# Gated linear attention plus a Fourier mix: rest rows stored in another order, z one step later, operands of the second product in other places

## The chip, the cores and the metric

The kernel runs on one core of a Trainium2 chip. The metric is device time in microseconds (us) of one execution. The engines are TensorE (PE; its weight loads are PEld), VectorE (DVE), ScalarE (ACT), GpSimd (POOL) and SyncE (SP, which only issues DMAs here; POOL issues some too).

## The reference

```python
x = A_x                                   # 1 x 2048 x 576
g = sigmoid((x * gate_w).sum(-1))         # a number per row
q, k, v = split(x @ wqkv)                 # 32 heads of 18
phi(t) = where(t > 0, t + 1, exp(t)) + 1e-6
kv  = phi(k)^T v ;  z = sum over rows of phi(k)
a   = ((phi(q) kv) / (phi(q) z + 1e-6)) @ wo
b   = dft_seq_re @ (B_x @ dft_hid_re^T) - dft_seq_im @ (B_x @ dft_hid_im^T)
out = g * a + (1 - g) * b                 # b uses x too (A_x)
```

`ORDER`, `PRODUCTS` and the "forms" below come from a scheme that multiplies 2 x 2 blocks with seven products instead of eight. All matmuls run in fp32r, each float32 operand split in a high part (`hi_of`, on ACT) and a low part (`lo_of`, on DVE), so that a product takes three passes (`FULL`).

## The kernel before

SBUF is one arena in which every tile has a byte address written by hand (`T_AT`, `ACC_AT`, `SLOT_AT`, ...). Where two tiles share bytes, the later writer waits until all readers of the earlier are done. SP runs in the order of the code, ACT and DVE from early in stage 1 on; PE's and POOL's order is chosen by the scheduler, PE's only up to the first product. Each DMA of SP takes one of eight lanes (a semaphore each, `DMAHW0` to `DMAHW7`) in turn, and waits until the DMA eight before it has landed.

The stages, with their places in the profiled execution:

1. k (0 to some 70 us): 16 row tiles of x times wk; `feature` gives k' in `acc[i]`, `pk[i]` holds its two parts. Beside it, `Left` makes the seven forms of x for the Fourier part, for 8 "pairs" of row blocks, and POOL stores them to DRAM (`xforms`, read back as `xf<-xm`). The 64 columns of x that don't fill a block of 128, the "rest", are made by `Left(NP)` for four pairs at once, in the two places g: a tile `plain` of 128 rows, q x r (32 rows of four pairs). SP stores it to `xrest` with six DMAs (L375), hi, hi and lo for each g; `load_rest` reads 96 rows of one pair (`xr<-xr`). This tile lies at `ACC_AT`, under `acc[0]` to `acc[5]`.
2. kv (to some 145 us): 20 steps (5 column chunks `c` of 4), each with 64 or 32 matmuls of `c` (x, loaded as `craw<-in_xg`) with `pk` (L599). Beside the steps: `zacc` sums k' over the tiles on DVE; `z_chain` splits the sum into `zs`, `z_sum` sums it over rows with four matmuls with `ones` (L197, tiles `zs`, `ones`) into `zb`; `kv_step` multiplies `gt` with `wv` (L581, L584); the five parts of `wo` are loaded (`wo_at`, one of them at the place of `zs`) and split; `wq` is loaded and split.
3. q (to some 226 us): 16 calls of `q_tile`: x times wq (28 matmuls, L197, tiles `wd`, `xs`), `feature` writes `acc[i]` (DVE, L331), and the next x is loaded (`xraw`, L247) and split (`xs`). After tile 1 `build_kv` masks kv; after tile 3 `build_m` multiplies it with `wo` into M (`mf`), all five groups; `move_m` brings M's rows to their places by POOL DMAs in the steps i = 4 to 6; `split_m` splits it after tiles 9 and 10. `wr_pieces` makes the forms of the Fourier weights.
4. attention (to 293.7 us): q' is normalised, transposed and multiplied with M; POOL stores `att`; the last forms of x are made (`Left(0)`, `Left(1)`, `Left(7)`), and `first` loads weights and x.
5. First product, `Hidden.run` (293.7 to 348.4 us): 8 pairs x 7 products x 7 matmuls (L857; the seventh is the rest). The results go to `Factors`, one of eight places `pair[p]` = `T_AT + p * TPAIR` for pair p. `load_x(p, k)` loads x's forms in four parts, `follow` says beside which pair's products the x of a later pair is loaded. `m.load(0)` loads the first 2 x 128 rows of the sequence matrix (`craw`), of which DVE and ACT make forms during pair 3.
6. First sequence (348.4 to 527.1 us): 32 steps `n` = (j, b), 168 matmuls each on average (L1018): matrix forms `c` with factors; step b uses pairs 2b and 2b + 1. `row` tiles (`att`) are loaded for each j, mixed, and stored (`mid`). `late(n)` makes the second weights and, in the last steps, starts the second product's loads.
7. Second product (527.1 to 587.3 us) and second sequence (to the end), with the imaginary matrices; `mid` takes the place of `att`, `out` that of `mid`.

The class `Layout` holds the addresses of the sequence matrix's batches, of x (`x`), rests (`rest`) and weights (`w`) for both products; `swap` is 1 for the second.

Of the kernel before, what the change touches and what calls it, by code (L numbers as in the profile page):

```python
# [8 lines left out]
F = mybir.dt.float32  # L9
# [5 lines left out]
P = 128  # L15
# [73 lines left out]
class Layout:  # L89
# [4 lines left out]

    def __init__(self, swap):
        self.swap = swap
        a, b = (2, 0) if swap else (0, 2)
        slot = [SLOT_AT + k * SLOT for k in range(7)]
        self.low = [slot[k] for k in (a + 1, b + 1, 4, 6)]
        self.high = [slot[k] for k in (a, b, 5)]  # L100

    def batch(self, n):

        if n == 0:
            return [T_AT + p * TPAIR for p in (NP - 2, NP - 1)]
        return self.low[(n - 1) % 4], self.high[(n - 1) % 3]

    def x(self, p, k):
        if 2 <= p <= 4:
            return T_AT + (4 * TPAIR, 7 * TPAIR, 4 * TPAIR + 7 * XF + XR)[p - 2] + k * XF  # L110
        return SLOT_AT + (p + self.swap) % 2 * 7 * XF + k * XF

    def rest(self, p):
        if p == 2:
            return T_AT + 4 * TPAIR + 7 * XF
        if p == 3:
            return T_AT + (NP - 2) * TPAIR + TPAIR // 2
        if p == 1 and not self.swap:
            return T_AT + 60416
        return WF_AT + 4 * WF if p % 2 else SLOT_AT + 14 * XF + 3 * WF  # L120

    def w(self, k):
        return WF_AT + k * WF if k < 4 else SLOT_AT + 14 * XF + (6 - k) * WF


@with_exitstack
def kernel(
# [209 lines left out]
    class Left:  # L337
# [18 lines left out]
        def make(self):  # L356

            r, c = self.f[:, :, 1], self.c
            add(r[:, 0], r[:, 1], r[:, 6])
            add(r[:, 4], r[:, 2], r[:, 6], ALU.subtract)  # L360
            yield
            add(r[:, 3], r[:, 0], r[:, 2], ALU.subtract)
            add(r[:, 6], r[:, 5], r[:, 3], ALU.subtract)
            yield
            hi_of(c[:, :4, 0], r[:, :4])
            hi_of(c[:, 4:, 0], r[:, 4:])
            yield
            for fs in (slice(0, 4), slice(4, 7)):
                lo_of(c[:, fs, 1], r[:, fs], c[:, fs, 0])
                if self.k < NP:  # L370
                    nc.gpsimd.dma_start(out=xforms[self.k][:, fs], in_=c.bitcast(F)[:, fs])
                yield
            for j in range(0 if self.k < NP else 6):
                k, g = j // 2, j % 2
                nc.sync.dma_start(out=xrest[g, :, k], in_=self.plain.bitcast(F)[:, g, k // 2])  # L375

    lefts = []

# [211 lines left out]
    for c in range(5):  # L590
        ps = [bank(), bank()]
        passes = FULL if c < KC else FULL[:2]
        for q in range(NCU):
# [129 lines left out]
        for o, s in todo:  # L723
            lo_of(o[:, :, 1], s, o[:, :, 0])

    def build_m():
        for g in range(NG):
# [90 lines left out]
    class Hidden:  # L818
# [38 lines left out]
                nc.tensor.matmul(ps, a, b, start=(start and n == 0), stop=(n == len(ops) - 1),  # L857
                                 skip_group_check=True)

        def run(self, m):  # L860
            rest = None

            follow, follow_rest = {0: 4, 2: 5, 3: 6, 5: 7}, {0: 4, 1: 5, 4: 6, 5: 7}
            self.load_rest(3)
            self.load_pair(3)
            for p in range(NP):
                fs = Factors(T_AT + p * TPAIR)
                factors.append(fs)
                t = fs.raw
                ys = (y_ring.next() for _ in range(3))  # L870
                if p == 0 and self.lay.swap:
                    o = self.lay.rest(3) + XR
                    ys = range(o, o + 3 * HALF * 4, HALF * 4)
# [202 lines left out]
    for i in range(NT):  # L1076
# [41 lines left out]
    def late(n):  # L1118
        k, part = divmod(n - 4, 7)
        if 0 <= k < 3 and part != 1:  # L1120
            go(wi_pieces[k])
        if 24 <= n < 28:
            second.load_w(n - 24)
        if n == 28:
            second.load_rest(1)
        if n == NP * NB - 3:
            second.load_rest(0)
            second.load_x(0, 4)
            second.load_x(0, 6)
            second.load_x(1, 0)  # L1130
        if n == NP * NB - 2:
            second.load_x(0, 0)
            second.load_x(0, 2)
            second.load_w(4)
        if n == NP * NB - 1:
            second.load_w(5)
            second.load_w(6)
            second.load_rest(2)
            for k in (2, 4, 6):
                second.load_x(1, k)  # L1140
# [19 lines left out]
def _layouts(inputs):  # L1160
# [14 lines left out]
    def left(xt):  # L1175
# [61 lines left out]
```

## Time and profile before

| what | us |
|---|---|
| median of 3 runs (lowest, highest) | 772.09 (768.91, 773.06) |
| profiled execution, own time | 771.09 |
| its span, first to last instruction | 769.4 |
| PE busy in the span | 732.4 |
| DVE, ACT, POOL busy | 600.7, 336.0, 56.7 |
| mean granted clock of PE (1 is full) | 0.980 |
| first product, second product | 54.7, 60.1 |

Rows of the timeline read: start, length, engine, line, operation, tiles; in brackets the idle time of the engine ahead of it and what ended that. Rows of waits: who waited for whom, us in total, times, longest. Rows of stretches: busy time and instructions of PE, PEld, DVE, ACT and POOL, then the granted clock, the busy share of the 16 DMA engines, and GB/s. Line numbers are those of the kernel before.

### The profile page before, as it was taken

The page shows a single profiled execution, that of the slowest core. Times are in us where ns is not written, and L with a number is a line of the kernel's source. Part 1 is how long each engine was busy: PE and PEld are TensorE (multiplying, and loading weights), DVE is VectorE, ACT ScalarE, POOL GpSimd, SP SyncE. Part 2 cuts the span into 40 slices and gives each one's busy share as a digit, 9 for nine tenths or more (in the row PEclk, how much of TensorE's full clock was granted, in tenths as well). Part 3 has the DMA queues.
Part 4 walks back from the last instruction along what each step waited for, and adds up shares of the span by engine and source line. Part 5 has one row for each costly group of instructions (what it writes and reads, how often), then busy time and mean ns, then how long its engine had stood idle before and what let it go on. Part 6 is the DMA issues. An engine that isn't in the chain of part 4 may idle for free.

```text
span 769.4 us, 13840 instructions
## 1 busy us (share of the span) xinstructions
PE 732.4 (95%) x5428; PEld 727.6 (95%) x5428; DVE 600.7 (78%) x993; ACT 336.0 (44%) x518; POOL 56.7 (7%) x98
## 2 busy tenths in 40 slices
PE   7999998539999999999999999999899999999998
PEld 7999998539999999999999999999889999999998
DVE  5789865236999985789998889885688987878885
ACT  6888435327864444435332424222343423333321
POOL 0111300005103211000001010000000000000000
PEclk9999999859999999999999999999999999999999
DMA  5476875226747797964547484868994354454441
GB/s 180 141 263 216 288 277 176 100 97 203 225 154 231 277 342 254 350 202 172 167 148 260 163 278 162 271 225 312 365 305 164 113 170 147 129 157 148 152 144 48
DMA packets 53724, 157.21 MB, mean 204 GB/s; under 512 B 6364, under 2 KB 10908, under 8 KB 52636
## 3 DMA queue, kind: packets, MB, share of 16 engines
q1 hardware_dynamic: 44412, 117.28, 46.4%
q0 software_dynamic: 8960, 38.65, 14.2%
q8 instruction: 43, 0.70, 0.4%
q10 hardware_dynamic: 288, 0.41, 0.1%
q14 instruction: 21, 0.17, 0.1%
HBM read 113.44 MB, written 41.39 MB: 201 GB/s over the span
## 4 chain that ended last, share of the span: by engine, by line
PE 71%; DMA 10%; DVE 2%; SPq 2%; issue 1%; ACT 0%; DVEq 0%; ACTq 0%
PE bank L1018 46%; PE bank L197 16%; PE bank L857 6%; DMA xf<-xm 4%; DMA xr<-xr 2%; DMA xraw<-in_xa_dram 2%; DMA mid<-row 1%; PE bank L695 1%; PE bank L599 1%; SPq L375 1%; DMA wraw<-in_wv_dram 1%; DMA xm<-xb 1%; SPq L247 1%; DVE fl L177 1%; DVE fl L187 0%
## 5 line engine op out<-in xcount | busy, mean ns | idle before, releaser
L1018 PE MATMUL bank<-fh,c 128*128 128x288 f32 x1792 | 357.6, 295 | 0.0
L1018 PEld LDWEIGHTS bank<-fh,c 128*128 128x128 f32 x1792 | 287.6, 188 | 0.0
L1018 PE MATMUL bank<-fl,c 128*128 128x288 f32 x896 | 264.4, 295 | 0.0
L167 ACT ACTIVATE c<-craw 128x1792 fp32r<-128x1792 f32 (+1 forms) x84 | 121.4, 1447 | 189.6 <-DVE craw L187 161.0
L1018 PEld LDWEIGHTS bank<-fl,c 128*128 128x128 f32 x896 | 168.9, 189 | 0.1
L197 PE MATMUL bank<-wd,xs 128*128 128x288 f32 (+1 forms) x896 | 128.1, 305 | 24.7 <-DVE acc L331 19.4
L197 PEld LDWEIGHTS bank<-wd,xs 128*128 128x128 f32 x896 | 125.2, 196 | 26.2 <-DVE acc L331 19.6
L177 DVE TENSOR_TENSOR c<-craw,c 128x1792 fp32r<-128x1792 f32 (+4 forms) x86 | 142.0, 1654 | 3.8 <-ACT c L167 3.6
L187 DVE TENSOR_TENSOR craw<-craw 128x256 f32<-128x256 f32 (+1 forms) x192 | 98.3, 512 | 34.1 <-DMA craw<-in_ci_dram 19.4
L857 PE MATMUL bank<-wf,xf 128*128 128x288 f32 x588 | 93.9, 300 | 4.1 <-ACT y L888 2.4
L857 PEld LDWEIGHTS bank<-wf,xf 128*128 128x128 f32 x588 | 84.8, 191 | 6.0 <-ACT y L888 3.0
L197 PE MATMUL bank<-mw,qs 128*128 128x288 f32 x448 | 63.3, 298 | 0.0
L599 PE MATMUL bank<-pk,c 128*128 128x288 f32 x448 | 62.7, 301 | 0.0
L331 DVE SCALAR_TENSOR_TENSOR acc<-bank,e 128x288 f32<-128x288 f32 x64 | 28.3, 454 | 43.4 <-DMA xraw<-in_xa_dram 23.1
L599 PEld LDWEIGHTS bank<-pk,c 128*128 128x128 f32 x448 | 61.3, 193 | 0.1
L197 PEld LDWEIGHTS bank<-mw,qs 128*128 128x128 f32 x448 | 60.0, 188 | 0.2 <-DVE qs L177 0.2
L187 DVE TENSOR_TENSOR ys<-bank,ys 128x288 f32<-128x288 f32 x63 | 28.8, 457 | 16.1 <-PE bank L1018 12.9
L167 ACT ACTIVATE fh<-fl 128x864 fp32r<-128x864 f32 (+1 forms) x32 | 29.8, 950 | 26.4 <-DVE fl L187 26.4
L329 ACT ACTIVATE e<-bank 128x288 f32<-128x288 f32 x64 | 25.9, 405 | 34.6 <-DVE acc L331 19.5
L177 DVE TENSOR_TENSOR fl<-fl,fh 128x864 fp32r<-128x864 f32 (+1 forms) x32 | 34.6, 1093 | 7.1 <-ACT fh L167 5.9
L857 PE MATMUL bank<-wf,xr 96*128 96x288 f32 x112 | 33.7, 301 | 2.3 <-DMA xr<-xr 2.3
L1083 ACT ACTIVATE acc<-bank,gate 128x288 f32<-128x288 f32 x32 | 16.0, 502 | 35.1 <-PE bank L197 34.8
(101 smaller groups left out, 622.0 us busy)
## 6 DMA issues: line engine op xcount, KB each, us to landing
xf<-xm SPq DMA_DIRECT2D x42, 512.0 KB
craw<-in_cr_dram SPq DMA_DIRECT2D x32, 512.0 KB
craw<-in_ci_dram SPq DMA_DIRECT2D x32, 512.0 KB
xraw<-in_xa_dram SPq DMA_DIRECT2D x31, 320.0 KB
xm<-xb POOLq DMA_DIRECT2D x8, 1024.0 KB, 5.4
wf<-wm SPq DMA_DIRECT2D x14, 576.0 KB
xm<-xb POOLq DMA_DIRECT2D x8, 768.0 KB, 5.5
xr<-xr SPq DMA_DIRECT2D x16, 336.0 KB
```

Source lines behind the costliest of these rows:

```text
L167: return nc.scalar.activation(dst, src, AF.Copy, bias=bias)
L177: nc.vector.tensor_tensor(out=dst, in0=src, in1=hi, op=ALU.subtract)
L187: nc.vector.tensor_tensor(out=dst, in0=a, in1=b, op=op)
L197: nc.tensor.matmul(ps, a, b, start=(n == 0), stop=(n == len(pairs) - 1))
L247: nc.sync.dma_start(out=raw, in_=xa[order.pop(0)])
L329: nc.scalar.activation(e, ps, AF.Relu, scale=-1.0)
L331: nc.vector.scalar_tensor_tensor(dst, ps, 0.0, e, op0=ALU.max, op1=ALU.add)
L375: nc.sync.dma_start(out=xrest[g, :, k], in_=self.plain.bitcast(F)[:, g, k // 2])
L599: nc.tensor.matmul(ps[h][:, :HALF], t[:, a, k], pk[s][:, b, half(h)], start=(s == 0 and n == 0), stop=(s == NT - 1 and n == len(passes) - 1))
L857: nc.tensor.matmul(ps, a, b, start=(start and n == 0), stop=(n == len(ops) - 1), skip_group_check=True)
L1018: nc.tensor.matmul(ps[q], c[x][:, l, k], factors[p](y, f), start=(p == 0 and i == 0), stop=(p == NP - 1 and i == 2))
L1083: done.append(nc.scalar.activation(acc[i][:, half(h)], ps[:, :HALF], AF.Copy, scale=gate[:, i:i + 1]))
```

## The change

Seven edits:

- Rest rows: x's rest is laid out so that a row of SBUF is r x q instead of q x r (the host gives `in_xq`'s rest block in that order), and the six stores write the same `xrest` with r as the outermost dimension.
- `z_chain` stands at the head of step 15's extra work instead of behind it; `z_sum`, the splits of `wo` and its loads come one step later.
- `Layout`: the same slots for the batches in both sequences; x's places in one table `xs`. In the second product x of pairs 0 to 4 lies in `pair[1]` to `pair[5]`, the places of the factors of the next pair; in the first, pairs 0 and 1 as before in the slots, 2, 3 and 4 in `pair[4]`, `pair[7]`, `pair[5]`. Rests get eight places: two of them beside what lies in `pair[6]`, one in `pair[7]`, the others in the ring of `row` tiles, behind the weights, and in slot 4.
- `late`: the second product's loads begin at step 27 (rest 0) and 28 (x of pair 0) instead of 28 and 29; in the last step x of the pairs 2 to 4, the rests up to 6 but 5, and `mi.load(0)` are put in SP's queue.
- First product: rest 2, x 3, rest 3, `mr.load(0)` and rest 4 stand ahead of the run. `follow` and `follow_rest` are given by the caller.
- The first two `wo` splits that were left are done in a loop behind `q_tile(0)`.
- `build_m` in three parts: groups 0 and 1 after tile 3, 2 and 3 after tile 4, 4 after tile 5.

```diff
 class Layout:
     def __init__(self, swap):
...
-        a, b = (2, 0) if swap else (0, 2)
         slot = [SLOT_AT + k * SLOT for k in range(7)]
-        self.low = [slot[k] for k in (a + 1, b + 1, 4, 6)]
-        self.high = [slot[k] for k in (a, b, 5)]
+        self.low, self.high = [slot[k] for k in (3, 1, 4, 6)], [slot[k] for k in (2, 0, 5)]
+        pair = [T_AT + p * TPAIR for p in range(NP)]
+        self.first = pair[6], pair[7]
+        self.xs = pair[1:6] if swap else [slot[0], slot[2], pair[4], pair[7], pair[5]]
+        self.xs += [slot[0], slot[2], slot[0]]
+        far, near = WF_AT + 4 * WF, slot[4]
+        self.sums = pair[7] + SLOT + XR
+        self.rests = [MIX_AT if p in (1, 7) else pair[6] + SLOT + (p - 2) * XR if p in (2, 3) else
+                      pair[7] + SLOT if p == 6 else far if p in ((0, 5) if swap else (4,)) else near
+                      for p in range(NP)]
...
     def x(self, p, k):
-        if 2 <= p <= 4:
-            return T_AT + (4 * TPAIR, 7 * TPAIR, 4 * TPAIR + 7 * XF + XR)[p - 2] + k * XF
-        return SLOT_AT + (p + self.swap) % 2 * 7 * XF + k * XF
+        return self.xs[p] + k * XF
...
-                nc.sync.dma_start(out=xrest[g, :, k], in_=self.plain.bitcast(F)[:, g, k // 2])
+                nc.sync.dma_start(out=xrest[g, :, k].rearrange("q r f n -> r q f n"),
+                                  in_=self.plain.bitcast(F)[:, g, k // 2])
...
+            if step == NT - 1:
+                z_chain()
             if q == 1 and c:
                 kv_step(c - 1)
...
-            elif step == NT - 1:
-                z_chain()
-            if step == NT:
+            if step == NT + 1:
                 z_sum()
-            if step >= NT:
+            if step > NT:
                 wo_split.pop(0)(lo_later)
-            if NT - 2 <= step < NT + 3:
-                g = step - NT + 2
+            if NT - 1 <= step < NT + 4:
+                g = step - NT + 1
...
-    wo_split.pop(0)()
+    for f in wo_split:
+        f()
...
-    build_m()
+    build_m((0, 1))
     for i in range(4, NT):
         q_tile(i)
+        build_m({4: (2, 3), 5: (4,)}.get(i, ()))
...
-            follow, follow_rest = {0: 4, 2: 5, 3: 6, 5: 7}, {0: 4, 1: 5, 4: 6, 5: 7}
-            self.load_rest(3)
-            self.load_pair(3)
...
-                    if p == 1 and k == 3:
-                        m.load(0)
...
-    hidden.load_rest(2)
...
         if 24 <= n < 28:
             second.load_w(n - 24)
+        if n == 27:
+            second.load_rest(0)
         if n == 28:
+            second.load_pair(0)
+        if n == 29:
+            second.load_pair(1)
             second.load_rest(1)
-        if n == NP * NB - 3:
...
+        if n == 30:
             second.load_w(4)
-        if n == NP * NB - 1:
             second.load_w(5)
+        if n == 31:
             second.load_w(6)
             second.load_rest(2)
+            second.load_rest(4)
             second.load_pair(2)
+            second.load_pair(3)
+            second.load_rest(3)
+            mi.load(0)
+            second.load_pair(4)
+            second.load_rest(6)
...
-    first.run(mr)
+    first.load_rest(2)
+    first.load_pair(3)
+    first.load_rest(3)
+    mr.load(0)
+    first.load_rest(4)
+    first.run(mr, {0: 4, 1: 5, 2: 6, 6: 7}, {0: 5, 3: 6, 4: 7})
...
-    second.run(mi)
+    second.run(mi, {1: 5, 2: 6, 6: 7}, {0: 5, 1: 7})
...
-        rest = rest.transpose(3, 1, 0, 2, 4).reshape(1, P, 4, 2 * P)
+        rest = rest.transpose(1, 3, 0, 2, 4).reshape(1, P, 4, 2 * P)
```

Where the order moves, engine by engine (line, operation, out<-in with numbers that tell tiles apart, size; in brackets the semaphores that an instruction waits for, where shown). First SP at the end of the kv stage, the loads of `wo` (L561) and the rest stores (L375), before:

```order
L561 DMA wraw_1541<-in_wo_dram 126x576
L498 DMA craw_1572<-in_xg_dram 128x512
L561 DMA wraw_1581<-in_wo_dram 126x576
L561 DMA wraw_1623<-in_wo_dram 126x576
L561 DMA wraw_1659<-in_wo_dram 126x576
L561 DMA wraw_1684<-in_wo_dram 72x576
L375 DMA xr_102<-xb_1223 4x32x896 x6
```

and after:

```order
L495 DMA craw_1569<-in_xg_dram 128x512
L558 DMA wraw_1578<-in_wo_dram 126x576
L558 DMA wraw_1611<-in_wo_dram 126x576
L558 DMA wraw_1654<-in_wo_dram 126x576
L558 DMA wraw_1679<-in_wo_dram 126x576
L371 DMA xr_102<-xb_1223 32x4x896 x6
L558 DMA wraw_1708<-in_wo_dram 72x576
```

The stores' shape changes from 4x32x896 to 32x4x896, and the last `wo` load moves behind them. DVE at the start of the q stage, where `acc_78` is `acc[0]`, before:

```order
L177 TENSOR_TENSOR gt_1712<-bank,gt_1712 128x288 [waits Activation_49] x2
L331 SCALAR_TENSOR_TENSOR acc_78<-bank,e_1744 128x288 [waits DMAHW2_49,DMAHW3_49,DMAHW1_49,DMAHW6_49,DMAHW0_49,DMAHW7_49,DVE_49,Activation_49]
L331 SCALAR_TENSOR_TENSOR acc_78<-bank,e_1764 128x288 [waits PE_49,Activation_49]
L653 TENSOR_SCALAR gate_75<-gate_75 128x1
L654 RECIPROCAL gate_75<-gate_75 128x1 [waits DVE_49]
L177 TENSOR_TENSOR xs_904<-xraw_905,xs_904 128x640 [waits Activation_49]
```

Nothing moves here: after the change the same instruction waits for six DMA lanes too. ACT at the end of the sum of k', before:

```order
L167 ACTIVATE c_1490<-craw_1488 128x512
L167 ACTIVATE plain_1502<-wraw_1503 128x576
L167 ACTIVATE zs_954<-zacc_953 128x576
L167 ACTIVATE xb_1223<-xb_1222 128x4x2x128
L167 ACTIVATE xb_1223<-xb_1222 128x3x2x128
```

and after:

```order
L163 ACTIVATE c_1490<-craw_1488 128x512
L163 ACTIVATE zs_954<-zacc_953 128x576
L163 ACTIVATE plain_1502<-wraw_1503 128x576
L163 ACTIVATE xb_1223<-xb_1222 128x4x2x128
L163 ACTIVATE xb_1223<-xb_1222 128x3x2x128
```

`zs` moves ahead of `plain` (the last chunk of `wv`). SP in the second product, from the load of x of pair 3 (`xm_97`) on, before:

```order
L833 DMA xr_6139<-xr_102 96x896
L840 DMA xf_6141<-xm_97 128x1024
L840 DMA xf_6143<-xm_97 128x1024
L840 DMA xf_6145<-xm_97 128x1024
L840 DMA xf_6147<-xm_97 128x512
L840 DMA xf_6176<-xm_98 128x1024
L840 DMA xf_6194<-xm_98 128x1024
L840 DMA xf_6214<-xm_98 128x1024
L840 DMA xf_6226<-xm_98 128x512
L833 DMA xr_6231<-xr_102 96x896
L954 DMA craw_6278<-in_ci_dram 128x1024
```

and after, where rest 4 (`xr_6118`) already stands ahead of x of pair 2:

```order
L839 DMA xf_6128<-xm_97 128x1024
L839 DMA xf_6130<-xm_97 128x1024
L839 DMA xf_6132<-xm_97 128x1024
L839 DMA xf_6134<-xm_97 128x512
L832 DMA xr_6136<-xr_102 96x896
L947 DMA craw_6138<-in_ci_dram 128x1024
L839 DMA xf_6140<-xm_98 128x1024
L839 DMA xf_6142<-xm_98 128x1024
L839 DMA xf_6144<-xm_98 128x1024
L839 DMA xf_6146<-xm_98 128x512
L832 DMA xr_6148<-xr_102 96x896
```

`craw` and the rest of pair 4 move ahead of x of pair 4 (`xm_98`).

More of the change, by code (lines that the diff above doesn't have):

```diff
@@ L96, in __init__ @@
         self.swap = swap
-        a, b = (2, 0) if swap else (0, 2)
         slot = [SLOT_AT + k * SLOT for k in range(7)]
-        self.low = [slot[k] for k in (a + 1, b + 1, 4, 6)]
-        self.high = [slot[k] for k in (a, b, 5)]
+        self.low, self.high = [slot[k] for k in (3, 1, 4, 6)], [slot[k] for k in (2, 0, 5)]
[8 more added lines that the diff above has]
+                      for p in range(NP)]
     def batch(self, n):
-        if n == 0:
-            return [T_AT + p * TPAIR for p in (NP - 2, NP - 1)]
-        return self.low[(n - 1) % 4], self.high[(n - 1) % 3]
+        return (self.low[(n - 1) % 4], self.high[(n - 1) % 3]) if n else self.first
     def x(self, p, k):
-        if 2 <= p <= 4:
-            return T_AT + (4 * TPAIR, 7 * TPAIR, 4 * TPAIR + 7 * XF + XR)[p - 2] + k * XF
-        return SLOT_AT + (p + self.swap) % 2 * 7 * XF + k * XF
+        return self.xs[p] + k * XF
     def rest(self, p):
[L114 to L120, printed above, removed]
+        return self.rests[p]
     def w(self, k):
-        return WF_AT + k * WF if k < 4 else SLOT_AT + 14 * XF + (6 - k) * WF
+        return WF_AT + k * WF if k < 4 else SLOT_AT + 14 * XF + XR + (6 - k) * WF
 @with_exitstack
@@ L724, in build_kv, with build_m @@
             lo_of(o[:, :, 1], s, o[:, :, 0])
-    def build_m():
-        for g in range(NG):
+    def build_m(gs):
+        for g in gs:
             n = gsize(g)
@@ L858, in product, with run @@
                                  skip_group_check=True)
-        def run(self, m):
+        def run(self, m, follow, follow_rest):
             rest = None
-            follow, follow_rest = {0: 4, 2: 5, 3: 6, 5: 7}, {0: 4, 1: 5, 4: 6, 5: 7}
-            self.load_rest(3)
-            self.load_pair(3)
             for p in range(NP):
@@ L871, in run @@
                 if p == 0 and self.lay.swap:
-                    o = self.lay.rest(3) + XR
-                    ys = range(o, o + 3 * HALF * 4, HALF * 4)
+                    ys = range(self.lay.sums, self.lay.sums + 3 * HALF * 4, HALF * 4)
                 p3, p2, e = (at(o, [P, HALF], F, "y") for o in ys)
@@ L1123, in late @@
             second.load_w(n - 24)
+        if n == 27:
+            second.load_rest(0)
         if n == 28:
+            second.load_pair(0)
+        if n == 29:
+            second.load_pair(1)
             second.load_rest(1)
-        if n == NP * NB - 3:
[L1127 to L1133, printed above, removed]
+        if n == 30:
             second.load_w(4)
-        if n == NP * NB - 1:
             second.load_w(5)
+        if n == 31:
             second.load_w(6)
             second.load_rest(2)
-            for k in (2, 4, 6):
-                second.load_x(1, k)
+            second.load_rest(4)
             second.load_pair(2)
-    paced.enter_context(tc.manual_schedule(engines={mybir.EngineType.PE}))
-    first.run(mr)
+            second.load_pair(3)
[3 more added lines that the diff above has]
+            second.load_rest(6)
+    paced.enter_context(tc.manual_schedule(engines={mybir.EngineType.PE}))
+    first.load_rest(2)
[4 more added lines that the diff above has]
+    first.run(mr, {0: 4, 1: 5, 2: 6, 6: 7}, {0: 5, 3: 6, 4: 7})
     sequence(mr, gate_n, att, mid, between=late)
     factors.clear()
-    second.run(mi)
+    second.run(mi, {1: 5, 2: 6, 6: 7}, {0: 5, 1: 7})
     sequence(mi, gate_m, mid, [out[t * P:(t + 1) * P] for t in range(NT)], last=gate_n)
```

## The prediction

> **What bounds the kernel now.** I read the page first, then who TensorE waited for, then busy time and clock by stretch, and then the order of time at each wait found.
>
> ```profile
> span 769.4 us, 13840 instructions
> PE 732.4 (95%) x5428; PEld 727.6 (95%) x5428; DVE 600.7 (78%) x993; ACT 336.0 (44%) x518; POOL 56.7 (7%) x98
> PEclk9999999859999999999999999999999999999999
> PE bank L197 <- DVE acc L331: 19.4, 1, 19.4
> ```
>
> TensorE is the bound: 95% busy, so only its 37 us of idle time and the time at a lower clock (eighth and ninth slice) can be won. Over half of the idle time is one wait of 19.4 us for the first write of `acc` in the q stage. The stretches around it (us; busy PE, PEld, DVE, ACT, POOL; clock; DMA share; GB/s):
>
> ```profile
> 128.00:131.40 3.40, 3.40 (x16) 3.40 (x16) 2.97 (x6) 2.14 (x6) 0.00 (x0) 0.51 0.02 9
> 145.90:165.40 19.50, 0.08 (x2) 0.05 (x1) 0.56 (x2) 0.07 (x1) 0.00 (x0) 0.57 0.37 140
> 165.40:172.40 7.00, 6.51 (x25) 6.15 (x26) 6.46 (x20) 3.88 (x11) 0.00 (x0) 0.50 0.02 7
> 172.40:176.00 3.60, 3.60 (x28) 3.60 (x28) 2.43 (x7) 2.40 (x6) 0.00 (x0) 0.99 0.30 91
> 144.00:146.00 2.00, 1.93 (x17) 1.70 (x15) 0.00 (x0) 1.32 (x4) 0.00 (x0) 1.00 0.26 106
> 318.00:320.00 2.00, 2.00 (x17) 2.00 (x16) 0.38 (x2) 0.41 (x1) 0.00 (x0) 1.00 1.01 262
> 298.00:300.00 2.00, 2.00 (x17) 2.00 (x16) 1.17 (x3) 0.41 (x1) 0.00 (x0) 1.00 1.05 422
> xr<-xb SPq DMA_DIRECT2D x6, 448.0 KB
> 132.92 15.37 SPq L375 DMA_DIRECT2D xr<-xb  x6
> 164.84 0.82 DVE L331 SCALAR_TENSOR_TENSOR acc<-bank,e 128x288 f32<-128x288 f32 x2 [23.15 <-DMA xraw<-in_xa_dram]
> ```
>
> From 145.9 to 165.4 no engine works; only DMAs run. SP issues the six rest stores (L375) from 132.92 on, and while they run alone (144 to 146) the DMA share is 0.26 of 16 engines, four engines, at 106 GB/s. 6 x 448 KB are 2.75 MB, 26 us at that rate, which fits the end of the wait. DVE's wait is labelled `xraw`, but its instruction in the order names six DMA lanes, those of the six stores: their source lies where `acc[0]` is written. After the idle time the clock is 0.50 until 172.4.
>
> **The change, part by part.**
>
> *A, the rest stores.* In the stretch 145.90 to 165.40 TensorE loses 19.4 us. From 165.40 to 172.40 it issues 25 matmuls; at the 28 in 3.60 us of the next stretch these take 3.2 us, so 3.8 us go to half clock and a last short wait. Together 23.2 us. What is late next: with the destination's outermost dimension 32 instead of 4, I take the stores to spread over 16 engines. Between the bounds of 106 GB/s (nothing won) and 422 GB/s (the stretch at 298, where POOL's stores of the forms run) I take the upper end, because both are stores from SBUF in rows of 3.5 KB and longer: 2.75 MB take about 7 us. The first store can't go before the fourth `wo` load, which waits for the last `zs` matmul, so about 131.5 by the times of part B; issue and completion are put at 2 us, an estimate from the rest load of part D (0.34 MB in 3.06 us), so the stores land near 141. TensorE needs the first `acc` only behind the second q tile, at 145.9 less part B's 1.8, near 144; DVE's write takes 0.8, so 2 us are spare and I count no rest. At 262 GB/s, the stretch at 318, the slowest with the DMAs full, the stores land near 144 and leave 1 to 2 us of wait: 21 us is A's lower end. The sixth `wo` transfer now stands behind the stores, and ACT's split of it ahead of the second tile's exponential; it is 162 KB, under 1 us after the stores, and its reader is the last third of M, over 10 us later, but ACT is blocked until then: the same 2 us cover it.
>
> The Trainium skill (DMA: Bandwidth & Descriptors, section Why a DMA increments its semaphore by 16 and not by 1) says that a copy is split over the largest number up to 16 that divides the slowest dimension of both sides. By that rule 4 and 128 give four engines, as the 0.26 shows, and 32 and 128 give 16; were it not so, A would be near 0 and the time near 761.
>
> *B, the sum of k'.*
>
> ```profile
> 123.86 0.63 ACT L167 ACTIVATE c<-craw 128x512 fp32r<-128x512 f32 x1 [4.41 <-DMA craw<-in_xg_dram]
> 125.30 0.68 ACT L167 ACTIVATE plain<-wraw 128x576 fp32r<-128x576 f32 x1 [0.81 <-DMA wraw<-in_wv_dram]
> 125.89 0.67 ACT L167 ACTIVATE zs<-zacc 128x576 fp32r<-128x576 f32 x1
> 126.61 0.40 PE L197 MATMUL bank<-zs,ones 128*128 128x288 f32 x1 [1.93 <-ACT zs L167]
> 127.74 3.92 PE L599 MATMUL bank<-pk,c 128*128 128x288 f32 x16
> 129.24 0.82 DVE L177 TENSOR_TENSOR gt<-bank,gt 128x288 fp32r<-128x288 f32 x2
> 131.77 0.28 PE L581 MATMUL bank<-gt,plain 128*126 128x252 f32 x1
> ```
>
> ACT's `zs` now stands ahead of `plain`, which waits for a load until 125.30. So it starts at 124.5 instead of 125.89, and both `zs` parts, and TensorE's 16 matmuls at 127.74, come 1.3 us sooner, without the half clock of 128 to 131.4 if the idle time falls enough. Then they end at 128.6; the next work, `gt` times `plain`, needs `gt`'s low part, whose place on DVE is unchanged (129.24 plus half of 0.82). TensorE starts there at 129.65 instead of 131.77, less 0.3 us for two `zs` matmuls that now stand behind: 1.8 us. If the clock still falls, half of 129.65 to 131.4 is lost: 0.9. That is decided by how much idle time a stretch of 3.4 us bears:
>
> ```profile
> 555.00:558.00 3.00, 0.66 (x6) 0.42 (x5) 0.00 (x0) 0.00 (x0) 0.00 (x0) 1.00 1.03 267
> 558.00:561.50 3.50, 3.40 (x15) 3.05 (x14) 1.86 (x5) 0.07 (x1) 0.00 (x0) 0.52 1.02 313
> 323.00:325.00 2.00, 1.19 (x9) 1.19 (x10) 1.86 (x4) 1.88 (x4) 0.00 (x0) 1.00 1.04 407
> ```
>
> About 2.3 us of idle time at 555 halved the clock for the next 3.5 us; about 1 us at 323 did not. Part B leaves about 1.3 us, nearer to the second, so I take 1.8. The Trainium skill (TensorE: Matmul & The Clock Gate, Part 1) puts the fall after a whole idle window of about 3.4 us; the trace disagrees, it fell after 2.3. By that rule B could not lose its 0.9; the sum is 1.8 either way.
>
> *C, the second product's operands.* The chain of waits (start, length) gives both products and their pace, the page's waits the cause:
>
> ```profile
> 293.68 13.65 PE bank L857 x103
> 307.33 11.53 DMA xr<-xr
> 348.35 178.78 PE bank L1018 x1344
> 527.13 4.67 PE bank L857 x35
> 573.00 14.24 PE bank L857 x105
> 587.25 175.43 PE bank L1018 x1320
> 530.00:535.00 5.00, 4.21 (x32) 4.00 (x31) 2.85 (x7) 1.34 (x2) 0.00 (x0) 1.00 1.03 346
> 529.62 4.56 SPq L840 DMA_DIRECT2D xf<-xm  x7
> 557.74 0.40 PE L857 MATMUL bank<-wf,xr 96*128 96x288 f32 x1 [2.34 <-DMA xr<-xr]
> 547.83 0.32 SPq L833 DMA_DIRECT2D xr<-xr  x1
> 559.60 0.69 DVE L187 TENSOR_TENSOR craw<-craw 128x512 f32<-128x512 f32 x1 [6.53 <-DMA craw<-in_ci_dram]
> ```
>
> A product is 8 x 49 = 392 matmuls; at 14.24 us for 105 that is 53.2. The second takes 587.25 - 527.13 = 60.1, so 6.9 us too long; the first 348.35 - 293.68 = 54.7, 1.5 too long. In the second, `xr` of pair 4 is issued at 547.83, since its place is free only after pair 2, and lands at 557.7 behind the loads of x; DVE waits for `craw` until 559.6 and holds banks back; then the clock is halved as shown. After the change, pairs 0 and 1 come while the sequence's last four steps run (their places are factors which these steps have used), some 2 MB more than now; rest 4 and `craw` stand ahead of x of pair 4 and wait for nothing later than the sequence's end. From 527.1 on SP has to bring 0.7 MB of weights, the rests 2 and 4 and x 2 (2.5 MB), x 3 with rest 3 and `craw` (2.7), x 4, at 1.8 MB for x and 0.34 for a rest. At the middle of 346 (the stretch at 530) and 422 GB/s these land by 536, 543 and 548, at 346 by 537, 544 and 550, against 540, 547 and 553 where TensorE wants pairs 2, 3 and 4. So C is the 6.9, at least 4 if the slow 267 GB/s stretch comes back. SP waits for TensorE's last step with all of it behind; x 2 went at 529.6 before and was in time.
>
> *D, the first product.* `craw` goes ahead of x 4: the 1.5 us of wait, which begin with DVE held at `craw`, go (0.3 if DVE's extra work alone causes them). But rest 2 now lies beside the forms of pair 7 and waits for their store:
>
> ```profile
> 289.88 13.10 SPq L833 DMA_DIRECT2D xr<-xr  x2
> 303.03 4.00 SPq L840 DMA_DIRECT2D xf<-xm  x8
> 567.33 3.06 DMA xr<-xr
> ```
>
> Of the two rests there, 3 is held by that store now, and went near 302.6, right ahead of the eight loads. Rest 2 now goes there instead of at 289.88; it is wanted at 307.8 (pair 2, seventh matmul), and a rest with little ahead of it took 3.06 us: 305.7, so 2.1 us are spare.
>
> *Edits at nothing.* M in three parts:
>
> ```profile
> 176.29 4.13 PE L197 MATMUL bank<-plain,kvb 126*126 126x288 f32 x30
> 180.26 11.90 PE L197 MATMUL bank<-wd,xs 128*128 128x288 f32 x88
> ```
>
> Its 30 matmuls and the tile behind them show no wait, so nothing can be won; the last parts of M move one and two q tiles back, by up to 7.2 us at 28 matmuls in 3.6, and POOL's moves of the later groups go behind two loads. M is split three tiles, 11 us, after its last move. Without that cover it would cost what is late, under 2 us. The `att` and `mid` rows now wait for the product's end; they are read four steps of 178.78 / 32 = 5.6 us later.
>
> Sum: 23.2 + 1.8 + 6.9 + 1.5 = 33.4, from the profiled execution's 771.1 to 737.7. The median shown stands 1.0 higher, so I say 738.
>
> **Rivals.**
>
> 1. The stores are late still, or DVE and ACT pile up behind them. For it: DVE was 6.46 of 7.00 us busy in the stretch after the wait. Against: TensorE ran on through it at half speed, and now has 2 us of lead. 3 to 8 us: 741 to 746.
> 2. The loads of the second product stay short: DMA share is 1.02 or more there, and the bytes are the same. C falls to 2: 743.
> 3. Rest 2 in the first product lands as late as the one at 307.33 did (11.53 us): 314.1, a wait of 6.3 and half clock after it, 1.7: 746. Against: eight loads stood ahead of that one, none of this.
> 4. The change of shape doesn't spread the stores: A is 0, 761.
> 5. Slower than before: each store writes four neighbouring rows to four places far apart in DRAM. If that scatter, not the engines, sets the rate, `acc[0]` waits longer than now. With B, C and D's 10.2 us kept, it turns slower when the stores last over 26 + 10 = 36 us, under 76 GB/s; at half the present rate it gives 787. Against: the runs stay 3.5 KB each, and four engines alone gave 106.
>
> **How the numbers follow.** As forecast (733 to 741) 0.64; rival 1 0.12; rival 2 0.12; rival 3 0.06; rival 4 0.04; rival 5 0.02. The range reaches from 733 (the three runs lie 3 us below to 1 above their median, D and C in full) to 747 (rivals 1 to 3), leaving out about 1 in 10. About 0.5%, 4 us, is what a measurement tells from no change: faster 0.96, same 0.02, slower 0.02.
>
> **What would show it.** A: DMA share near 1 during the stores, no wait of `acc` over 1 us, clock 1.00 from 132 on. B: `zs` matmuls by 125.5. C and D: both products 53 to 54 us, no wait for `xr`. Wrong if `acc` still waits long, if a new wait for `plain` or `xs` takes its place near 143 to 155, or if the second product stays near 60.

## Result, and the profile after

| | before | after |
|---|---|---|
| median, us (lowest to highest) | 770.50 (767.16 to 773.06, 4 runs) | 740.88 (737.97 to 744.29, 4 runs) |
| ratio after / before | | 0.962 [0.9554, 0.9685] |
| profiled execution, own time, us | 771.09 | 738.69 |
| its span, us | 769.4 | 737.0 |

30 us were won; predicted were 33, to 738. One run of "after, again" below, 749.71 us, is a slow one: the median given for it is that of its five other runs, 0.9601 of before, while the ratio of 0.9629 beside it may count the slow one. From the page and the waits of TensorE after:

```profile
span 737.0 us, 13853 instructions
PE 724.3 (98%) x5428; PEld 721.4 (98%) x5428; DVE 600.7 (82%) x993; ACT 335.7 (46%) x518; POOL 57.0 (8%) x98
PEclk9999999999999999999999999999999999999999
PE bank L193 <- DVE xs L173: 3.9, 1, 3.9
PE bank L856 <- DMA xr<-xr: 3.0, 1, 3.0
```

The wait of 19.4 us at `acc` is gone, and so is the dip of the clock in the eighth and ninth slice. The largest wait left, 3.9, stands at the kernel's start and was there before. The second, 3.0 us for a rest (`xr`) in the first product, is new. (In after, L193 is the old L197, L856 the old L857, L1011 the old L1018, L327 the old L331, L371 the old L375.)

First the place of the stores and of the sum of k': the timeline, and below it busy time by stretch (columns as in the prediction):

```profile
122.61 0.67 ACT L163 ACTIVATE zs<-zacc 128x576 fp32r<-128x576 f32 x1
124.12 0.40 PE L193 MATMUL bank<-zs,ones 128*128 128x288 f32 x1 [0.40 <-DVE zs L173]
124.46 2.39 PE L596 MATMUL bank<-pk,c 128*128 128x288 f32 x16
126.54 0.82 DVE L173 TENSOR_TENSOR gt<-bank,gt 128x288 fp32r<-128x288 f32 x2
127.05 0.38 PE L578 MATMUL bank<-gt,plain 128*126 128x252 f32 x1 [0.21 <-DVE gt L173]
128.61 5.83 SPq L371 DMA_DIRECT2D xr<-xb  x6
140.08 0.82 DVE L327 SCALAR_TENSOR_TENSOR acc<-bank,e 128x288 f32<-128x288 f32 x2 [3.93 <-DMA xraw<-in_xa_dram]
```

```profile
130.00:134.00 4.00, 4.00 (x32) 4.00 (x31) 3.92 (x7) 1.70 (x4) 0.00 (x0) 1.00 1.01 402
134.00:140.00 6.00, 6.00 (x49) 6.00 (x48) 0.82 (x2) 3.57 (x9) 0.00 (x0) 1.00 0.94 328
```

The six stores are issued within 6 us, the DMA share is 1.01 and 0.94 instead of 0.26, and DVE writes the first `acc` at 140.08, with TensorE busy all the time (6.00 of 6.00 us in the second stretch). The 16 `pk` matmuls behind `zs` take 2.39 instead of 3.92 us: the clock no longer falls there.

Then the products: the chain of waits, the stretch behind the new wait with its clock, and SP's part of the timeline:

```profile
266.29 4.69 PE bank L856 x35
284.77 13.01 DMA xf<-xm
297.85 11.63 DMA xr<-xr
309.52 14.10 PE bank L856 x92
323.62 178.74 PE bank L1011 x1344
502.36 4.69 PE bank L856 x35
508.44 47.19 PE bank L856 x350
```

```profile
309.90:313.30 3.40, 3.40 (x17) 3.40 (x16) 0.45 (x1) 1.63 (x3) 0.00 (x0) 0.50 0.38 143
```

```profile
283.52 0.32 SPq L832 DMA_DIRECT2D xr<-xr  x1
284.77 12.32 SPq L839 DMA_DIRECT2D xf<-xm  x8
297.85 1.56 SPq L832 DMA_DIRECT2D xr<-xr  x2
```

The second product runs without a break, 53.3 us (502.36 to 555.6). The first takes 57.3 (266.29 to 323.62): at 306.5 TensorE stops at pair 6's seventh matmul for a rest issued at 297.85, right behind the eight loads of x of pairs 5 and 6, and after 3 us of wait the clock is 0.50 for 3.4 us. So by stages of the two profiled executions: up to the first product 27.4 us won, first product 2.7 lost, second product 6.9 won, the rest 0.8; together 32.4.

### The profile page after: what moved, and what is told of

It is laid out like the page before. It is cut to its first block, busy times and chain, and to the rows that moved or that the text cites. A ratio compares the mean times of both kernels' runs of the same rounds, so it can differ in the third digit from the quotient of the medians.

```text
span 737.0 us, 13853 instructions
## 1 busy us (share of the span) xinstructions
PE 724.3 (98%) x5428; PEld 721.4 (98%) x5428; DVE 600.7 (82%) x993; ACT 335.7 (46%) x518; POOL 57.0 (8%) x98
## 4 chain that ended last, share of the span: by engine, by line
PE 74%; DMA 7%; DVE 2%; ACT 1%; issue 0%; SPq 0%; DVEq 0%; ACTq 0%
PE bank L1011 46%; PE bank L193 17%; PE bank L856 10%; DMA xr<-xr 3%; DMA xf<-xm 2%; PE bank L692 1%; DVE fl L173 1%; DMA craw<-in_ci_dram 1%; DMA xm<-xb 1%; DMA craw<-in_xg_dram 1%; PE bank L596 1%; DVE c L173 1%; DVE craw L183 0%; DVE row L1027 0%; ACT xb L163 0%
## 5 line engine op out<-in xcount | busy, mean ns | idle before, releaser
L1011 PE MATMUL bank<-fh,c 128*128 128x288 f32 x1792 | 356.2, 295 | 0.0
L1011 PEld LDWEIGHTS bank<-fh,c 128*128 128x128 f32 x1792 | 287.1, 188 | 0.0
L1011 PE MATMUL bank<-fl,c 128*128 128x288 f32 x896 | 264.2, 295 | 0.3 <-DVE fl L173 0.3
L1011 PEld LDWEIGHTS bank<-fl,c 128*128 128x128 f32 x896 | 168.8, 188 | 0.7 <-DVE fl L173 0.5
L193 PE MATMUL bank<-wd,xs 128*128 128x288 f32 (+1 forms) x896 | 124.1, 299 | 4.7 <-DVE xs L173 3.9
L193 PEld LDWEIGHTS bank<-wd,xs 128*128 128x128 f32 x896 | 121.5, 191 | 5.7 <-ACT wd L163 4.6
L856 PE MATMUL bank<-wf,xf 128*128 128x288 f32 x588 | 93.6, 300 | 0.5 <-DVE fl L173 0.5
L856 PEld LDWEIGHTS bank<-wf,xf 128*128 128x128 f32 x588 | 85.3, 192 | 0.7 <-DVE fl L173 0.7
L193 PE MATMUL bank<-mw,qs 128*128 128x288 f32 x448 | 63.2, 297 | 0.0
L596 PE MATMUL bank<-pk,c 128*128 128x288 f32 x448 | 60.9, 296 | 0.0
L193 PEld LDWEIGHTS bank<-mw,qs 128*128 128x128 f32 x448 | 59.9, 188 | 0.2 <-DVE qs L173 0.2
L327 DVE SCALAR_TENSOR_TENSOR acc<-bank,e 128x288 f32<-128x288 f32 x64 | 28.2, 453 | 19.6 <-ACT e L326 15.3
L856 PE MATMUL bank<-wf,xr 96*128 96x288 f32 x112 | 33.7, 301 | 3.0 <-DMA xr<-xr 3.0
```

The costliest lines, as they stand in the source:

```text
L193: nc.tensor.matmul(ps, a, b, start=(n == 0), stop=(n == len(pairs) - 1))
L327: nc.vector.scalar_tensor_tensor(dst, ps, 0.0, e, op0=ALU.max, op1=ALU.add)
L596: nc.tensor.matmul(ps[h][:, :HALF], t[:, a, k], pk[s][:, b, half(h)], start=(s == 0 and n == 0), stop=(s == NT - 1 and n == len(passes) - 1))
L1011: nc.tensor.matmul(ps[q], c[x][:, l, k], factors[p](y, f), start=(p == 0 and i == 0), stop=(p == NP - 1 and i == 2))
```

## Experiments

Twelve runs in three groups, each group on one chip with its own runs of the kernel before (medians 770.66, 771.84, 770.12).

| kernel | median, us | ratio to before [95%] |
|---|---|---|
| after, again | 739.92 | 0.9629 [0.9587, 0.9672] |
| rest 6 early | 736.75 | 0.9556 [0.9531, 0.9581] |
| after, z as before | 742.74 | 0.9640 [0.9609, 0.9670] |
| after, M whole | 742.32 | 0.9622 [0.9595, 0.9648] |
| before, rows only | 749.52 | 0.9713 [0.9694, 0.9732] |
| before, four stores for one | 752.40 | 0.9747 [0.9723, 0.9771] |
| after, small loads behind | 740.62 | 0.9608 [0.9564, 0.9652] |
| after, second product as before | 777.57 | 1.0080 [1.0054, 1.0106] |
| rest 6 early, again | 737.38 | 0.9582 [0.9556, 0.9608] |
| rest 6 early, row tiles free | 737.31 | 0.9577 [0.9550, 0.9605] |
| rest 6 early, pair 1 late | 741.63 | 0.9632 [0.9610, 0.9653] |
| rest 6 early, both late | 743.16 | 0.9649 [0.9626, 0.9672] |

A change of 1 or 2 us is hardly seen in such times, so the stages of the profiled executions are set beside them (us, between the first matmuls of the stages, each start rounded to 0.1; one execution for each kernel):

| kernel | to first product | first product | first sequence | second product | to the end |
|---|---|---|---|---|---|
| before | 293.5 | 54.7 | 178.8 | 60.1 | 182.3 |
| after | 266.1 | 57.4 | 178.7 | 53.2 | 181.6 |
| after, again | 267.5 | 54.3 | 179.6 | 52.7 | 182.6 |
| rest 6 early | 266.4 | 52.8 | 177.7 | 53.2 | 183.0 |
| z as before | 269.4 | 53.7 | 180.3 | 53.5 | 183.2 |
| M whole | 266.9 | 57.1 | 180.0 | 55.0 | 182.5 |
| rows only | 269.2 | 55.2 | 179.3 | 60.6 | 182.3 |
| four stores | 274.2 | 55.0 | 177.8 | 61.6 | 182.7 |
| small behind | 267.9 | 52.7 | 179.2 | 54.8 | 182.6 |
| second as before | 266.6 | 85.1 | 179.7 | 60.4 | 182.2 |
| rest 6 early, again | 266.7 | 52.9 | 179.0 | 52.9 | 182.6 |
| row tiles free | 266.8 | 54.8 | 178.6 | 56.5 | 182.3 |
| pair 1 late | 266.6 | 53.0 | 180.8 | 58.2 | 182.8 |
| both late | 266.9 | 52.6 | 178.8 | 59.7 | 182.5 |

**After, again.** No edit.

> The changed kernel again, beside the three edits of it below, on one chip. Expected 0.962 of the kernel before, about 741 us; TensorE's one wait of some 3 us for a rest in the first product stands again.

739.92 us, 0.9601 by the medians. The wait for the rest was 1.6 us this time, not 3.0, and no half clock followed it; the second row of the waits and the stretch around it (clock 1.00) are for the last section:

```profile
PE bank L856 <- DMA xr<-xr: 1.6, 1, 1.6
PE bank L193 <- ACT zs L163: 0.8, 1, 0.8
```

```profile
121.00:134.00 13.00, 11.54 (x83) 10.68 (x82) 8.39 (x15) 9.46 (x18) 0.00 (x0) 1.00 0.71 239
```

So the wait is not one fixed size, and that may be part of why runs of the changed kernel spread over some 5 us.

**Rest 6 early.**

```diff
-MIX_AT if p in (1, 7) else
+MIX_AT if p in ((1, 7) if swap else (1, 6)) else
...
-far if p in ((0, 5) if swap else (4,)) else near
+far if p in ((0, 5) if swap else (4, 7)) else near
-first.run(mr, {0: 4, 1: 5, 2: 6, 6: 7}, {0: 5, 3: 6, 4: 7})
+first.run(mr, {0: 4, 1: 5, 2: 6, 6: 7}, {0: 5, 1: 6, 4: 7})
```

> In the first product rest 6 goes to the place of rest 1, free after pair 1, and is loaded ahead of x of pair 6; rest 7 goes to the place of rest 4. Theory 1 (the rest is late because its place, under x of pair 3, is free only after pair 3, when eight loads of x stand ahead of it in SP's queue): the wait of 3.03 us and the 3.4 us at half clock behind it (1.7 lost) both go, the first product takes 52.7 to 53.5 us instead of 57.3, the time falls by 4 to 4.6 us. Theory 2 (the DMA engines are full from 288 to 309, so somebody waits whatever the order): the wait passes to x of pair 6 or 7, and the time falls by less than 2 us.

Theory 1 holds in its mechanism: 736.75 against 739.92 us, 3.2 less. That is short of the 4 to 4.6 expected from a wait of 3.03 us, and the wait in after again was 1.6. The edit also takes rest 7 out from under the row tiles, so part of the 3.2 can lie in the first sequence. In the chain of waits the first product is one unbroken piece, and in the timeline rest 6 leaves at 291.98, ahead of x of pair 6:

```profile
266.58 52.73 PE bank L856 x392
```

```profile
285.50 5.46 SPq L839 DMA_DIRECT2D xf<-xm  x4
291.98 0.32 SPq L832 DMA_DIRECT2D xr<-xr  x1
294.31 3.76 SPq L839 DMA_DIRECT2D xf<-xm  x4
```

```profile
303.00:306.00 3.00, 3.00 (x25) 3.00 (x24) 2.97 (x7) 0.41 (x1) 0.00 (x0) 1.00 1.04 361
```

The DMA engines are as full as before (1.04, against 1.05 in the same stretch after), so theory 2 falls; the place in the queue decided. Five profiled executions with rest 6 in its old place (the one with the second product as before, whose first product another edit disturbs, left out) agree with it: issued 29.4 (small behind), 30.7 (z as before), 31.0 (after again), 31.7 (after) and 32.9 us (M whole) behind the first product's start, it was late by 0, 1.0, 1.6, 3.0 and 2.4 us: later with a later issue, but for the last.

**After, z as before.** `z_chain`, `z_sum`, the loads and splits of `wo` stand at their old steps.

```diff
-            if step == NT - 1:
-                z_chain()
...
+            elif step == NT - 1:
+                z_chain()
-            if step == NT + 1:
+            if step == NT:
                 z_sum()
```

> The changed kernel with z_chain, z_sum and the loads and splits of wo at their old steps. Theory 1 (DVE stands in order behind zs, so gt moved with it, and the half clock went): up to the first product 27.4 us were won, 23.2 by the stores, so this costs about 4.2 us. Theory 2 (the step as predicted, gt at its old time): 1.8 us. Theory 3 (the stores, again 4 us later, land after the first acc is wanted): 4.2 us and a new wait at acc of 1 to 3 us on top, 5 to 7 us.

The first product starts at 269.4, against 266.1 to 267.9 (mean 266.8) in the ten profiled executions with `z` as after: 2.6 us by this one execution, between theories 1 and 2. The wait and the half clock are back in the waits and the stretches, and no wait at `acc` appears, so theory 3 falls:

```profile
PE bank L193 <- ACT zs L163: 2.1, 1, 2.1
121.00:134.00 13.00, 10.54 (x69) 10.04 (x68) 6.49 (x11) 8.43 (x16) 0.00 (x0) 0.87 0.62 185
```

The whole time, 742.74, is 2.8 us over after again, with overlapping intervals.

**After, M whole.** `build_m(range(NG))` after tile 3, no later calls.

> The changed kernel with all five groups of M made after the fourth q tile. Theory 1: nothing, within 1 us, since these 30 matmuls showed no wait before the change. Theory 2: the part up to the first product that neither the stores nor the sum of k' explain (27.4 less 23.2 less 3.4, 0.8 us) comes from here, so 0.8 us slower; with a wait at M's evictions, up to 2.

Nothing is seen: 0.9622 [0.9595, 0.9648], with overlapping intervals, and 266.9 to the first product. The higher median, 742.3, is not told from 739.9; what this profiled execution has more lies in waits for loads in both products.

**Before, rows only.** The edit to the six stores and the host's order of the rest rows, in the kernel before.

> The kernel before with the rest rows alone changed (layout in SBUF and shape of the six stores). Theory 1 (the wait for acc was the time of stores on four engines): they are issued from 132.9 as before, take 11 us as in the changed kernel, land near 144, ahead of the first acc; the wait of 19.4 and 3.8 us at half clock go, 23 us, about 747.5 us (0.970). Theory 2 (the earlier sum of k' and the last wo load behind the stores were needed too): 1 to 3 us of the wait stay, 749 to 751.

749.52, 22.3 us less than before; 24.3 less up to the first product. No wait at `acc` is left, so theory 1 holds, though the time lies where theory 2 put it (749 to 751); the wait at `zs` and its half clock stay (0.87 in the stretch from 121 to 134), as they belong to part B.

```profile
131.40 6.02 SPq L375 DMA_DIRECT2D xr<-xb  x6
PE bank L197 <- ACT zs L167: 1.7, 1, 1.7
121.00:134.00 13.00, 10.91 (x71) 10.41 (x71) 7.06 (x12) 8.99 (x17) 0.00 (x0) 0.87 0.65 197
```

**Before, four stores for one.**

```diff
-nc.sync.dma_start(out=xrest[g, :, k], in_=self.plain.bitcast(F)[:, g, k // 2])
+for q in range(4):
+    nc.sync.dma_start(out=xrest[g, q, k],
+                      in_=self.plain.bitcast(F)[32 * q:32 * q + 32, g, k // 2])
```

> The kernel before, with its rows in place, but each of the six stores cut in four, one for each 32 rows (24 stores of 112 KB). Theory 1 (the outermost dimension of 4 held a store on four engines): each small store has 32 rows outermost and uses 16, the rate is 300 GB/s or more; SP issues 24 in some 15 us, so they land near 149, 3 us late: 18 to 21 us won, 750 to 753. Theory 2 (what mattered is where the rows lie, not the number of engines): the rate stays near 106 GB/s and the time near 771.

752.40, within theory 1's 750 to 753: with every row where it was, the stores spread. In the timeline SP needs 12.86 us to issue 24 of them, which at 2.75 MB is 214 GB/s, near the 200 measured, so the issues seem to set the rate, and TensorE waits a little at `acc`:

```profile
131.74 12.86 SPq L376 DMA_DIRECT2D xr<-xb  x24
139.00:144.00 5.00, 5.00 (x43) 5.00 (x41) 0.82 (x2) 3.92 (x11) 0.00 (x0) 1.00 0.76 200
PE bank L197 <- DVE acc L331: 1.9, 1, 1.9
```

The Trainium skill's rule on the spread (DMA: Bandwidth & Descriptors, Why a DMA increments its semaphore by 16 and not by 1) gives 16 engines here too, for 32 rows outermost; the share of 0.76 at 200 GB/s, against 0.26 at 106, agrees.

**After, small loads behind.** In the second product's queue `load_rest(4)` and `mi.load(0)` stand behind `load_pair(4)`.

> The changed kernel, but in the second product's queue rest 4 and craw stand behind x of pair 4 instead of ahead of x of pairs 2 and 4. Theory 1 (their order was most of the 6.9 us): rest 4 lands as late against its pair as before, 2.3 us of wait for it, DVE late at craw, half clock after: 4 to 6 us slower, 745 to 747. Theory 2 (x of pairs 0 and 1, loaded under the sequence, was most of it: the queue is 2 MB shorter, so all that is behind lands 6 us sooner): within 1 us of 740.5.

Theory 2: 740.62, no slower. The second product takes 54.8 instead of 53.2 us, 1.6 more. Of that, 0.7 is a wait in pair 4 where the kernel before waits 1.3:

```profile
PE bank L856 <- ACT y L881: 0.7, 1, 0.7
```

This is one execution, and the other kernels whose second product is that of after took 52.7 to 55.0 us for it (M whole the longest, with 1.7 us of wait for a weight), so the 1.6 is a hint and not a price.

**After, second product as before.** Places of x, rests and weights, `late` and `follow` of the second product as in the kernel before; the first sequence's batches and the first product's x of pairs 5 to 7 change slots with them.

> The changed kernel, but with the places, the order and the steps of the second product's loads as in the kernel before (and the slots of the first sequence's batches, which these places need). Theory 1 (the account by stages): the second product takes 60 instead of 53.3 us, 747 us. Theory 2 (part of it was lost again at the start of the second sequence, where craw now waits): only 4 to 6 us slower, 744.5 to 746.5.

The second product takes 60.4 us, as theory 1 has it. The total can't be used: x of pair 5 in the first product now shares its slot with pair 1 while it is asked for beside pair 1's products, and TensorE stands there for x (L866 is the product's line here):

```profile
PE bank L866 <- DMA xf<-xm: 26.4, 3, 19.7
266.70:351.70 85.00, 58.62 (x394) 57.74 (x393) 42.28 (x82) 22.15 (x38) 2.94 (x5) 0.80 0.54 175
531.40:591.80 60.40, 54.90 (x395) 53.64 (x394) 43.11 (x84) 21.44 (x37) 0.00 (x0) 0.97 0.88 301
```

So C is seen here in its stage alone. The last group tells the parts of C apart in another way, with rest 6 early as its base.

**Rest 6 early, again.**

> The kernel with rest 6 early once more, as the base of the three edits below on one chip. Expected 0.956 of the kernel before; no wait for a rest in the first product.

737.38 (0.9582), a first product of 52.9 us and no wait for a rest, as expected. No run of after stands beside it in this group; the ratio is below the 0.962 of the result, with overlapping intervals.

**Row tiles free.** In the second product rest 7 goes to slot 4, loaded beside pair 4.

> Rest 6 early, and in the second product rest 7 goes to slot 4 (the place of rest 4) instead of under the row tiles. Theory 1 (with a rest under the row tiles until the product's end, the first two row loads and the matrix loads behind them leave 0.8 us later, and TensorE waits 0.3 to 1.2 us for fl early in the sequence; with rest 6 early this wait was gone in the first sequence): 0.3 to 1 us faster than rest 6 early. Theory 2 (the matrix load waits for the product's end anyway): no difference.

0.9577 against 0.9582: no difference. Its profiled execution, 740.69, shows 1.7 us of wait for a weight in the second product and 1.0 for a rest in the first, which its base doesn't; M whole has the wait for the weight too, so such waits come and go from one execution to the next.

**Pair 1 late.** `load_pair(0)` one step later, `load_pair(1)` behind the last step's weights.

> Rest 6 early, but in the second product x of pair 0 is loaded one step later and x of pair 1 behind the sequence's last step, so that SP has 1.8 MB more to bring after that step. Theory 1 (C was the 2 MB brought under the sequence): 1.8 MB at 311 to 330 GB/s are 5.5 to 5.9 us; pair 1 is wanted 6.7 us after the start and lands after some 8 to 9, so the product takes 56 to 59 us instead of 53.2. Theory 2 (order of the small loads, which stays): 53 to 54 us.

Theory 1, by the times: the product takes 58.2 us, and the whole is 4.3 slower than its base. But x of pair 1 itself came in time. What came late is behind it in the queue: x of pair 2, 1.4 us, and the rest of pair 3, 2.3 us, with half clock after it.

**Both late.** As the last, with rest 4 and `craw` behind x of pair 4 too.

> As the one with pair 1 late, and rest 4 and craw behind x of pair 4 too. Theory 1 (both together are the 6.9 us of the second product): 59 to 61 us for the product, 5 to 8 us slower than rest 6 early. Theory 2 (they overlap: the small loads wait in the same queue, so the second costs nothing more): as with pair 1 late alone, within 1 us.

59.7 us, which is the old product's 60.1 but for 0.4; 743.16, 5.8 slower than the base. The waits and the stretches of these two in the second product:

```profile
PE bank L856 <- DMA xr<-xr: 2.3, 1, 2.3
PE bank L856 <- DMA xf<-xm: 1.4, 1, 1.4
500.40:558.60 58.20, 54.52 (x394) 54.05 (x393) 43.44 (x84) 21.84 (x37) 0.00 (x0) 0.97 0.90 306
PE bank L856 <- DMA xr<-xr: 2.7, 1, 2.7
498.30:558.00 59.70, 55.15 (x394) 53.97 (x393) 42.98 (x83) 21.44 (x37) 0.00 (x0) 0.97 0.90 298
```

## Why the prediction was right, and where not

- **A, the stores: right.** 23.2 us were forecast; rows only gave 22.3 by the times and 24.3 by the stages. The rate behind it, 422 GB/s taken from POOL's stores, was 402 and then 328 in the stretches of the stores. They were issued from 128.61 on, not 131.5, and the first `acc` was written at 140.08 with no wait of TensorE, where the prediction has it wanted near 144. Rivals 1, 4 and 5 fall, and rival 2 with C. Two readings of the prediction are off without harm to the sum: 26 us from 132.92 end at 158.9 and not at the wait's end, 164.84, for the sixth store was issued only at 144.1; and the `wo` load that moves behind the stores is the fifth of five, not the sixth.
- **B, the sum of k': right in sign, 0.7 us short.** Forecast 1.8, measured 2.6 (z as before) and 2.4 (rows only, 269.2, less 266.8). The step that missed is the one that held `gt` at 129.24 since "its place on DVE is unchanged". Its place in the order is, but DVE's `gt` needs the high part that ACT makes, and ACT makes it behind `plain`, `zs`, two `xb` and `wd`, without a pause. These began at 125.30 before, with `plain`, which waits for its load, and at 122.61 after, with `zs`. ACT's `gt` stands 3.3 us behind that in both, and just ahead of its own `gt` DVE waits for ACT (first row before, the others after):

```profile
128.62 0.69 ACT L167 ACTIVATE gt<-bank 128x288 fp32r<-128x288 f32 x2
125.92 0.69 ACT L163 ACTIVATE gt<-bank 128x288 fp32r<-128x288 f32 x2
126.05 0.46 DVE L173 TENSOR_TENSOR wd<-wraw,wd 64x290 fp32r<-64x290 f32 x1 [0.97 <-ACT wd L163]
```

So DVE's `gt` came to 126.54 in the profiled execution, 2.7 us sooner; on average it starts at 128.6 in the four executions with the old order and at 127.3 in the ten with the new, 1.3 sooner. Up to the first product the profiled executions of z as before and after lie 3.3 us apart; by the mean of the ten, 0.7 of that is chance.
- **C, the second product: right.** 6.9 forecast, 53.2 instead of 60.1 measured, 6.9. What the runs add: x of pair 1 behind the sequence, with pair 0 a step later, costs 5.2 us (58.2 less 53.0, the mean of the two bases), and the order of rest 4 and `craw` another 1.5 or 1.6, which is within what single executions differ. The prediction gave both and a price for neither; the shorter queue weighs more.
- **D, the first product: wrong.** Forecast were 1.5 us won. The step that failed is that on the rests: "Of the two rests there" it followed rest 2, whose place waits for a store, and that one was in time (issued at 273.63, no wait at pair 2). It didn't follow rest 6, whose new place lies under x of pair 3 and is free only after pair 3, when SP has the eight loads of x of pairs 5 and 6 ahead of it. That is rival 3's mechanism on another rest, and its own row, 11.53 us behind eight loads, gave the right size: 11.63. Over the five executions with rest 6 there the first product took 52.7 to 57.4 us, on average 55.0, and the three with the old first product 54.7 to 55.2, so D is about nothing instead of 1.5, with 2.7 lost in the profiled one. Rest 6 early shows that the gain was there: 52.8.
- **At nothing:** M in parts shows no difference, as said.
- **The sum.** By the stages A, B and C are 24.3 + 2.5 + 6.9 = 33.7, and D 0. The times give 30.7 (770.66 to 739.92 in the first group). That the forecast of 33.4 lies so near the 32.4 of the profiled pair is in part luck, since A and B brought more and D less. (Also, 1.0 on 737.7 is 738.7, not 738.) Of the 3 us between, part may lie in the first sequence: five executions of after and its edits with rest 6 in place took 178.7 to 180.3 there, on average 179.6, three with the old first product 177.8 to 179.3, 178.6. TensorE waits early in it for `fl`, 0.9 us in after again and 1.2 in z as before, behind a `craw` that leaves at the product's end. With rest 7 out from under the row tiles (rest 6 early and its four kin) this wait is gone in four executions of five, but pair 1 late has 1.8 us of it (180.8), so what sets it stays open.

The version with rest 6 early has the lowest times: 736.75 and 737.38 us, 0.9556 and 0.9582 of before.

## What to carry to other kernels

The wait here, at a DMA share that stood near a quarter, was for stores on four of 16 engines; where such a share shows, look at the shape of the outermost dimension before size or place. When operands get new places, follow every one of them, the smallest too: what its place waits for, how many loads stand ahead of it in the queue at that time, and at how many GB/s they leave; one row of a late small load in the trace prices all others of its kind. In the full queue here, bytes moved under an earlier stage were worth more than their order within it.

## What the runs showed of the hardware

A short wait can cost half as much again, or not, by its length and place. Half clock came in stretches of 3.41 us and multiples. On the grid that they make, from the clock's changes and TensorE's matmuls in all profiled executions: where TensorE, at full clock, was idle for 1.59 us or less of a 3.41 us window, the next was at full clock too; where it was 1.89 us or more, the next was at 0.5; between them 1.61 and 1.71 brought it down, 1.76 and 1.81 didn't. So in these runs the edge lies near half a window. The rows above show it at one place: with a wait of 0.8 us at `zs` the stretch had clock 1.00, with 1.7 and 2.1 it had 0.87. The Trainium skill (TensorE: Matmul & The Clock Gate, Part 1) has the window of 3.4 us, with which these lengths agree, but asks for a whole idle one before the clock falls, with which they don't. It shows in the first product as well: M whole, with 2.8 us of wait for rests, 2.4 of it in one piece, took 57.1 us; after again, with 1.6, took 54.3: 2.8 us more for 1.2 us more of wait. M whole's row:

```profile
PE bank L855 <- DMA xr<-xr: 2.8, 2, 2.4
```
